# Reordering two products of a seven-product matrix scheme, and one Silu over two PSUM banks in place of two

## The chip, the cores and the metric

The kernel runs on one core of a Trainium2 chip. TensorE (PE) multiplies into PSUM, VectorE (DVE) and ScalarE (ACT) read and write PSUM and SBUF, GpSimd (POOL) works on SBUF alone, and SyncE (SP) issues the DMAs. The engines run side by side. Each takes its own instructions in order, and they wait for each other through semaphores. The metric is the device time of one execution in microseconds (us), as the median of several runs.

## The reference

A bf16 input `x` of 2048 tokens by 512 features is normalised (`xn`). To `x` two things are added: a linear attention over 32 heads of 16 features, and a gated feed-forward block of width 1792. What matters here is the second:

```python
g = silu(xn @ w_gate)
u = xn @ w_up
y = (g * u) @ w_down
```

## The kernel before

The first 512 tokens go through plain matmuls for gate and up (`gu`, line 556). The other 1536 tokens, the part that matters here, go through a scheme with seven products in place of eight (Strassen's, in Winograd's form). The left operand is made of four blocks of the weights (two halves of the contraction of `w_gate` and of `w_up`); the right one is made of four blocks of the input (two halves of the contraction by two halves of 768 tokens). Some products take sums of blocks, made beforehand by DVE (`w_sums`, `x_sum`, line 808).

The loop at line 1132 runs over 14 steps `fc`, each for 128 of the 1792 hidden columns. A step treats the tokens of each block in two halves `q` of `TS` = 384. Each half owns three PSUM banks, `a, b, d = GB[q]`; banks 0 and 1 stay free for other work. A product (`prod`, line 846) is two matmuls of 384 columns into one of these banks. For each half the work is:

- product 1 into `a`; ACT copies `a` to `b` (`seed`, line 856), so that later products add on top of it
- product 5 into `d`; ACT copies `d` to an SBUF tile `p5` (`keep5`, line 861)
- product 2 added into `a`, which then is the gate of the first token block; ACT takes its Silu (`gate(q, 0)`, line 868)
- product 6 added into `b`; DVE writes `b` + `p5` into `d` (`u4`, line 874)
- product 3 added into `d`, the gate of the second block; ACT takes its Silu (`gate(q, 1)`, line 868 too)
- product 7 added into `b`; DVE writes `b` + `p5` to the tile `c22` (`up22`, line 879), and POOL multiplies that with the Silu (`h22`, line 883)
- product 4 added into `b`; DVE multiplies that with the Silu of the first block (`h21`, line 889)

In a step PE takes product 1 of both halves, then 5 of both, then 2, 6, 2, 6 (each half's pair in turn), then 2 fillers (`fill(FA)`), then 3, 7, 3, 7, then 3 fillers (2 in steps 2, 4, 6, 8, 12 and 13; `fill(FB...)`), then 4, 4. A filler is one 512-column matmul of the output of the first 512 tokens (lines 682 and 686).

Each engine's queue is written out in the order of the program text (`K.add`). A helper, `_Program`, finds the waits: an instruction waits for the last writer of all that it reads, and for the last writer and all readers of what it writes. A PSUM bank counts as a whole. So product 2 into `a` waits until `seed` has read `a`, and product 4 into `b` waits until `up22` has read `b`. `seed` of the next step, which writes `b`, waits until `h21` has read it.

After its two Silus of a step ACT has further work before the next step's `seed`: in steps 1 to 9 it scales a slice of `w_gate` or `w_up` (`SC`, line 800), in steps 2 to 7 it also makes a small [128, 1] scalar (`SMALL`, line 780), in steps 10 and 11 it copies part of `w_down` (line 997), and from step 11 it copies pieces of the hidden tile (`hcopy`, line 1055). POOL has, besides `h22`, the products of the attention's division (lines 654, 638), whose results SP turns with DMA transposes.

After step 13 the product with `w_down` uses the same scheme and the same bank triples (`dprod`, line 1083; `attn`, line 1089).

Of the kernel before, what the change touches and what calls it, by code (L numbers as in the profile page):

```python
# [6 lines left out]
ACT = mybir.ActivationFunctionType  # L7
ALU = mybir.AluOpType

P = 128  # L10
# [22 lines left out]
TB = (S - T0) // 2  # L33
TS = TB // 2
# [83 lines left out]
def bass_parallel_sum__linear_attn_block__swiglu_ffn__prompt_kernel(nc, A_x, A_wqkv, A_wo, B_x, B_w_gate, B_w_up, B_w_down, out):  # L118
    xin = A_x[0]
    oview = out[0]  # L120
    K = _Program()
    bf, f32 = dt.bfloat16, dt.float32

    with contextlib.ExitStack() as es:
        E = es.enter_context

        def sb(name, shape, dtype):
            return E(nc.sbuf_tensor(name, shape, dtype))
# [19 lines left out]
        zacc = sb("zacc", [P, 2, D], f32)  # L148
# [35 lines left out]
        sil4 = zacc[:, :, :].rearrange("p a b -> p (a b)").bitcast(bf)[:, 0:4 * TS].rearrange("p (n f) -> p n f", n=4)  # L184
# [12 lines left out]
        c22 = sb("c22", [P, 2, TS], f32)  # L197
# [4 lines left out]
        iw = sb("iw", [P, 2], f32)  # L202
# [8 lines left out]
        sx = sb("sx", [P, 1], f32)  # L211
        iso = sb("iso", [P, 1], f32)
        sm = sb("sm", [P, 1], f32)
        banks = [E(nc.psum_tensor("pb%d" % i, [P, 512], f32)) for i in range(8)]

        def B(i):
            return ("bank", i)
# [48 lines left out]
        for t in range(4, 16):  # L266
# [5 lines left out]
            out=ident[:, :], in_=ident[:, :], compare_op=ALU.not_equal, fill=1.0,  # L272
# [302 lines left out]
        def hj(fc):  # L575
            if fc < 9:
                return hTf[:, fc * HB:(fc + 1) * HB]
            return xnf[:, (fc - 9) * HB:(fc - 8) * HB] if fc < 12 else pqf[:, (fc - 12) * HB:(fc - 11) * HB]

        def hjold(fc):  # L580
            if fc < 9:
                return ph1
            if fc < 12:
                return [("xn", t) for t in range(3 * (fc - 9), 3 * (fc - 8))]
            return [("pq", t) for t in range(3 * (fc - 12), 3 * (fc - 11))]
# [242 lines left out]
                tt("dve", S_[2], A11, A21, ALU.subtract, gk + uk, [("S", n, 2)])  # L828
                tt("dve", S_[3], A12, S_[1], ALU.subtract, gk + [("S", n, 1)], [("S", n, 3)])

        GB = ((2, 3, 4), (5, 6, 7))

        def prod(q, fc, bank, i, start):
            p, o = fc // 2, (fc % 2) * P
            n = p % 2
            cs = slice(fc * P, (fc + 1) * P)
            ts = slice(q * TS, (q + 1) * TS)
            L = {1: wg[:, 0:2, cs], 2: wg[:, 2:4, cs], 4: wu[:, 2:4, cs]}
            lk = {1: ("wgc", fc), 2: ("wgc", fc), 4: ("wuc", fc)}
            for a, b in ((5, 0), (6, 1), (7, 2), (3, 3)):  # L840
                L[a], lk[a] = Sw[:, n, b, :, o:o + P], ("S", n, b)
            R = {1: B11, 2: B21, 3: B22, 4: Tx[3], 5: Tx[0], 6: Tx[1], 7: Tx[2]}
            lo = [("xnT", t) for t in range(4 + 3 * q, 7 + 3 * q)]
            hi = [("xnT", t) for t in range(10 + 3 * q, 13 + 3 * q)]
            rk = {1: lo, 2: lo, 3: hi, 4: [("T", 4)], 5: [("T", 1)], 6: [("T", 2)], 7: [("T", 3)]}
            K.add("pe", [(lambda e, c=c: e.matmul(  # L846
                banks[bank][:, 0:TS], L[i][:, c, :], R[i][:, c, ts], start=(start and c == 0), stop=(c == 1),
                skip_group_check=True)) for c in (0, 1)],
                r=[lk[i]] + rk[i], w=[B(bank)])

        def bk(i):
            return banks[i][:, 0:TS]

        def seed(q, fc):
            a, b, d = GB[q]
            K.add("act", lambda e: e.activation(bk(b), bk(a), ACT.Copy),  # L856
                  r=[B(a)] + ([("sil", 0), ("sil", 1)] if fc == 0 else []), w=[B(b)])

        def keep5(q):
            a, b, d = GB[q]  # L860
            K.add("act", lambda e: e.activation(p5[:, q, :], bk(d), ACT.Copy), r=[B(d)], w=[("p5", q)])

        seen = set()

        def gate(q, i):
            bank = GB[q][0] if i == 0 else GB[q][2]
            n = 2 * q + i
            K.add("act", lambda e: e.activation(sil4[:, n, :], bk(bank), ACT.Silu, scale=iw[:, 0:1]),  # L868
                  r=[B(bank), ("iw",)], w=[("sil4", n), ("zacc", 0), ("zacc", 1)] if n not in seen else [("sil4", n)])
            seen.add(n)  # L870

        def u4(q):
            a, b, d = GB[q]
            K.add("dve", lambda e: e.tensor_tensor(out=bk(d), in0=bk(b), in1=p5[:, q, :], op=ALU.add),  # L874
                  r=[B(b), ("p5", q)], w=[B(d)])

        def up22(q):
            a, b, d = GB[q]
            K.add("dve", lambda e: e.tensor_tensor(out=c22[:, q, :], in0=bk(b), in1=p5[:, q, :], op=ALU.add),  # L879
                  r=[B(b), ("p5", q)], w=[("c22", q)])  # L880

        def h22(q, fc):
            K.add("pool", lambda e: e.tensor_tensor(  # L883
                out=hj(fc)[:, TB + q * TS:TB + (q + 1) * TS], in0=c22[:, q, :], in1=sil4[:, 2 * q + 1, :], op=ALU.mult),
                r=[("c22", q), ("sil4", 2 * q + 1)], w=[("hj", fc, 2 + q)], a=hjold(fc))

        def h21(q, fc):
            b = GB[q][1]
            K.add("dve", lambda e: e.tensor_tensor(
                out=hj(fc)[:, q * TS:(q + 1) * TS], in0=bk(b), in1=sil4[:, 2 * q, :], op=ALU.mult),  # L890
                r=[B(b), ("sil4", 2 * q)], w=[("hj", fc, q)], a=hjold(fc))

        todo = []

# [232 lines left out]
        LATE = {10: [(11, 0)], 11: [(11, 1)]}  # L1127
        SMALL = {i + 2: [fn] for i, fn in enumerate(smalls_d())}
        FA, FB = 2, 3
        DIV = {i: ORDER[i] for i in range(11)}  # L1130
        TURN = {11: (8, 9), 12: (10,)}
        for fc in range(NFC):
            for q in (0, 1):
                prod(q, fc, GB[q][0], 1, True)
                seed(q, fc)
            if fc == 0:
                fill(4)
            for q in (0, 1):
                prod(q, fc, GB[q][2], 5, True)
                keep5(q)  # L1140
            for q in (0, 1):
                prod(q, fc, GB[q][0], 2, False)
                gate(q, 0)
                prod(q, fc, GB[q][1], 6, False)
                u4(q)
            p = fc // 2
            if fc == 0:
                den_sum(DIV[0])
            if fc in DIV:
                den_turn(DIV[fc])  # L1150
            if fc == 1:
                scales_d(1)
            if fc == 12:
                t1_part(0, 1)
                bcopy(22, 1, "pool", [("Tt", 1, 0, 1)])
            if fc == 13:
                t1_part(1, 1)
            fill(FA + (fc == 12))
            for q in (0, 1):
                prod(q, fc, GB[q][2], 3, False)  # L1160
                gate(q, 1)
                prod(q, fc, GB[q][1], 7, False)
                up22(q)
                h22(q, fc)
            fill(FB - (fc in (2, 4, 6, 8, 12)) if fc < 13 else 2)
            if fc == 6:
                oout(1, 1)
            if fc == 0:
                gather_d()
            for q in (0, 1):  # L1170
                prod(q, fc, GB[q][1], 4, False)
                h21(q, fc)
            if p + 1 < NPAIR:
                w_sums(p + 1, fc % 2)
            if fc == 0:
                scale("wu", 2, "pool", [("S", 1, 1)])
            for key, i in SC.get(fc, ()):
                scale(key, i)
            if fc == 0:
                total_d(1)  # L1180
            for fn in SMALL.get(fc, ()):
                fn()
            for n, s_ in LATE.get(fc, ()):
                bcopy(n, s_, "act")
            if fc == 11:
                t1_part(0, 0)
                bcopy(22, 0, "pool", [("Tt", 1, 0, 0)])
            for i in {11: (1,), 12: (0,), 13: (2, 3)}.get(fc, ()):
                hcopy(0, i)
            if fc == 12:  # L1190
                t_sum(2, 0)
                t1_part(1, 0)
                bcopy(21, 0, "pool", [("Tt", 1, 1, 0)])
                bcopy(21, 1, "pool")
            if fc == 13:
                h_sum(0, 0)
                h_sum(0, 1)
                t_sum(2, 1)
            if fc in DIV:
                pq_mul(DIV[fc], [("S", (p + 1) % 2, 1 + 2 * (fc % 2))] if p + 1 < NPAIR else [])  # L1200
                if SLOT[DIV[fc]] < 8:
                    turn(DIV[fc])
                pz_ahead(DIV[fc])
            for i in TURN.get(fc, ()):
                turn(ORDER[i])
            if fc in (9, 10):
                m_scale(fc - 9)
            if fc + 1 in DIV:
                den_sum(DIV[fc + 1])
# [21 lines left out]
        for p in range(NP2 - 1):  # L1231
            a, b, d = GB[p % 2]
# [121 lines left out]
```

## Time and profile before

| | |
|---|---|
| median of 3 runs (lowest, highest) | 200.51 us (200.50, 200.74) |
| the profiled execution, own time | 200.89 us |
| its span, first to last instruction | 199.6 us |
| granted TensorE clock | 1.00 |
| the 14 steps of the loop at line 1132 | 74.88 to 154.16 us |
| in 74.9 to 154.2: PE, DVE, ACT, POOL busy | 78.9, 69.6, 69.2, 57.9 of 79.3 us |

The span is cut into parts by the trace: the attention's projections up to 44.6 us, the plain gate and up products to 74.9 us, the 14 steps to 154.2 us, and the product with `w_down` after that. A busy PE means that some matmul was in flight. Matmuls overlap, so the distance from one matmul's start to the next one's tells more than the busy share. Two matmuls of a product start 0.1625 us apart, each is shown with 0.326 us, so a product takes 0.325 us of PE and its result is there 0.49 us after its start.

### The profile page before, as it was taken

What the parts mean: (1) busy time and instruction counts of PE and PEld (TensorE: products, weight loads), DVE (VectorE), ACT (ScalarE), POOL (GpSimd) and SP (SyncE); (2) the same over time, 40 slices, a digit from 0 to 9 for tenths busy, and PEclk for the clock granted to TensorE, in tenths of its full rate; (3) what the DMA queues carried; (4) which work ended last, traced back from release to release, by engine and by line L of the source; (5) the groups of instructions that cost most, each with busy time, mean ns of one, the idle gap of its engine ahead of it and who ended that gap; (6) DMA issues with size and microseconds to landing.
All of it is one profiled execution on the core that took longest, in us unless ns stands there. A gap on an engine that the chain in (4) does not pass through costs nothing.

```text
span 199.6 us, 3566 instructions
## 1 busy us (share of the span) xinstructions
PE 195.1 (98%) x1193; PEld 114.8 (58%) x1207; DVE 170.5 (85%) x339; ACT 153.6 (77%) x308; POOL 122.3 (61%) x150
## 2 busy tenths in 40 slices
PE   8899999999999999999999999999999999999995
PEld 2344444444544445555555555555555888888884
DVE  2999998894797798988888998887799999998866
ACT  3799887749889988689898988888989968475200
POOL 3687876799995544787677666768877004413220
DMA  6943243289990000011111221000210012132223
GB/s 180 355 122 81 57 87 73 50 282 364 375 295 3 0 3 0 0 28 31 26 26 26 53 56 23 4 0 7 45 34 0 3 39 66 30 79 66 45 69 118
DMA packets 28899, 15.97 MB, mean 80 GB/s; under 512 B 17232, under 2 KB 28880, under 8 KB 28880
## 3 DMA queue, kind: packets, MB, share of 16 engines
q1 hardware_dynamic: 28320, 15.28, 27.3%
q10 hardware_dynamic: 560, 0.46, 0.7%
q8 instruction: 9, 0.15, 0.3%
q14 instruction: 10, 0.08, 0.1%
HBM read 9.70 MB, written 2.10 MB: 59 GB/s over the span
## 4 chain that ended last, share of the span: by engine, by line
PE 94%; DVE 2%; DMA 2%; issue 1%; ACT 0%; POOL 0%; SPq 0%
PE pb L846 32%; PE pb L1083 16%; PE pb L431 13%; PE pb L556 12%; PE pb L480 7%; PE pb L682 6%; PE pb L1089 5%; PE pb L686 2%; DMA x_sb<-in_A_x_dram 2%; PE pb L605 1%; PE pb L674 0%; DVE pq L470 0%; PE pb L398 0%; POOL ef L459 0%; DVE stats L298 0%
## 5 line engine op out<-in xcount | busy, mean ns | idle before, releaser
L654 POOL TENSOR_TENSOR pq<-pq,rden 128x512 bf16<-128x512 bf16 x16 | 16.9, 1056 | 36.7 <-DVE rden L650 23.1
L868 ACT ACTIVATE zacc<-pb,iw 128x384 bf16<-128x384 f32 x56 | 31.3, 590 | 5.9 <-PE pb L846 4.7
L431 PE MATMUL pb<-wqkv,xnT 128*128 128x512 bf16 x110 | 25.1, 379 | 0.2
L846 PE MATMUL pb<-xnT,wg 128*128 128x384 bf16 x112 | 25.1, 326 | 0.0
L638 POOL TENSOR_TENSOR pz<-pq,zbc 128x512 f32<-128x512 bf16 x16 | 18.6, 1164 | 5.3 <-DVE ef L808 3.8
L883 POOL TENSOR_TENSOR hT<-c,zacc 128x384 bf16<-128x384 f32 x18 | 16.1, 915 | 6.0 <-DVE c L879 4.0
L459 POOL TENSOR_SCALAR ef<-ef 128x512 bf16<-128x512 bf16 x25 | 15.5, 620 | 5.8 <-ACT ef L452 5.6
L879 DVE TENSOR_TENSOR c<-pb,p 128x384 f32<-128x384 f32 x28 | 15.5, 555 | 4.1 <-PE pb L846 2.8
L431 PEld LDWEIGHTS pb<-wqkv,xnT 128*128 128x128 bf16 x112 | 10.9, 98 | 13.3 <-DVE pk L470 0.4
L452 ACT ACTIVATE ef<-pb 128x512 bf16<-128x512 f32 x25 | 14.8, 593 | 3.9 <-PE pb L431 3.9
L874 DVE TENSOR_TENSOR pb<-pb,p 128x384 f32<-128x384 f32 x28 | 15.3, 561 | 1.7 <-PE pb L846 0.9
L497 POOL TENSOR_TENSOR zacc<-zacc,pk 128x512 f32<-128x512 f32 x13 | 15.4, 1181 | 1.0
L856 ACT ACTIVATE pb<-pb 128x384 f32<-128x384 f32 x28 | 12.7, 473 | 3.8 <-PE pb L846 2.9
L846 PEld LDWEIGHTS pb<-xnT,wg 128*128 128x128 bf16 x112 | 10.6, 98 | 7.7 <-ACT pb L856 0.8
L556 PE MATMUL pb<-xnT,wg 128*128 128x512 bf16 x56 | 14.7, 379 | 0.0
L556 PE MATMUL pb<-xnT,wu 128*128 128x512 bf16 x53 | 14.3, 379 | 0.1
L846 PE MATMUL pb<-xnT,wqkv 128*128 128x384 bf16 x56 | 13.7, 326 | 0.0
L846 PE MATMUL pb<-GT,wqkv 128*128 128x384 f16 x56 | 13.7, 326 | 0.0
L846 PE MATMUL pb<-wo,wqkv 128*128 128x384 f16 x56 | 13.7, 326 | 0.0
L298 DVE BATCH_NORM_STATS2 stats<-x_sb 128x6 f32<-128x512 bf16 x16 | 10.8, 678 | 3.0 <-DMA x_sb<-in_A_x_dram 3.0
L1089 PE MATMUL pb<-M,pk 128*128 128x256 bf16 x96 | 13.4, 273 | 0.0
L480 PE MATMUL pb<-pk,xn 128*128 128x512 bf16 x55 | 12.5, 379 | 0.1
(210 smaller groups left out, 488.6 us busy)
## 6 DMA issues: line engine op xcount, KB each, us to landing
x_sb<-in_A_x_dram SPq DMA_DIRECT2D x14, 128.0 KB, 4.5
wg<-in_B_w_gate_dram SPq DMA_DIRECT2D x2, 896.0 KB, 8.3
wu<-in_B_w_up_dram SPq DMA_DIRECT2D x2, 896.0 KB, 9.6
wd<-in_B_w_down_dram SPq DMA_DIRECT2D x2, 896.0 KB, 13.7
out_dram<-out_sb SPq DMA_DIRECT2D x24, 64.0 KB, 1.6
wqkv<-in_A_wqkv_dram SPq DMA_DIRECT2D x3, 256.0 KB, 5.0
wqkv<-in_A_wqkv_dram SPq DMA_DIRECT2D x1, 512.0 KB, 9.0
wo<-in_A_wo_dram SPq DMA_DIRECT2D x1, 512.0 KB, 10.0
```

The lines of the kernel that those rows point to most:

```text
L431: K.add("pe", [(lambda e, c=c: e.matmul(banks[b][:, :], src[:, c, t * P:(t + 1) * P], wqkv[:, c, col:col + D], start=(c == 0), stop=(c == ...
L459: K.add("pool", lambda e: e.tensor_scalar(out=buf, in0=buf, scalar1=top, scalar2=0.0, op0=ALU.min, op1=ALU.max), r=[bkey] + tkeys, w=[bkey])
L480: K.add("pe", [(lambda e, c=c: e.matmul(banks[c][:, :], src[:, t, c * P:(c + 1) * P], pk[:, t, :], start=first, stop=last)) for c in range ...
L556: fns.append(lambda e, c=c, b=b, w_=w_: e.matmul(banks[b][:, :], w_[:, c, fc * P:(fc + 1) * P], xnT[:, c, C * 512:(C + 1) * 512], start=(c ...
L638: K.add("pool", lambda e: e.tensor_tensor(out=pzh[i][:, :, 0:DH], in0=heads(pq[:, t, :]), in1=heads(zbc[:, :]), op=ALU.mult), r=[("pq", t) ...
L654: K.add("pool", lambda e: e.tensor_tensor(out=heads(pq[:, t, :]), in0=heads(pq[:, t, :]), in1=rden[:, i, :][:, :, None].broadcast_to([P, N ...
L846: K.add("pe", [(lambda e, c=c: e.matmul(banks[bank][:, 0:TS], L[i][:, c, :], R[i][:, c, ts], start=(start and c == 0), stop=(c == 1), skip ...
L868: K.add("act", lambda e: e.activation(sil4[:, n, :], bk(bank), ACT.Silu, scale=iw[:, 0:1]), r=[B(bank), ("iw",)], w=[("sil4", n), ("zacc", ...
L879: K.add("dve", lambda e: e.tensor_tensor(out=c22[:, q, :], in0=bk(b), in1=p5[:, q, :], op=ALU.add), r=[B(b), ("p5", q)], w=[("c22", q)])
L883: K.add("pool", lambda e: e.tensor_tensor(out=hj(fc)[:, TB + q * TS:TB + (q + 1) * TS], in0=c22[:, q, :], in1=sil4[:, 2 * q + 1, :], op=AL ...
L1083: K.add("pe", [(lambda e, k=k: e.matmul(split(banks[b][:, 0:HD]), L[:, k, :], cut[:, :, k * P:(k + 1) * P], start=(start and k == 0), stop ...
L1089: K.add("pe", [(lambda e, g=g: e.matmul(dk(b), pk[:, SLOT[t], g * P:(g + 1) * P], M[:, g, lo:lo + HD], start=False, stop=(g == NG - 1), sk ...
```

## The change

Three things are done.

The banks are dealt out anew: half 0 has 2, 4, 6 and half 1 has 3, 5, 7, where they had 2, 3, 4 and 5, 6, 7. The eight PSUM tensors of one bank each become one tensor of eight banks, so that an instruction can name two neighbouring ones.

The Silu of the first token block becomes one instruction for both halves (`gate2(0)`), which reads banks 2 and 3 and writes two neighbouring pieces of `sil4`. It stands behind product 2 of half 1. The Silu of the second block stays one for each half (`gate1(q)`). The pieces of `sil4` are numbered anew.

In steps 0 to 11 (`FS = 12`), and in half 1 only (`SWAP = (1,)`), product 7 and `up22` stand ahead of product 3 and its Silu. PE's order there is 3, 7, 7, 3 in place of 3, 7, 3, 7. In steps 12 and 13 it stays.

```diff
-        banks = [E(nc.psum_tensor("pb%d" % i, [P, 512], f32)) for i in range(8)]
+        psum = E(nc.psum_tensor("pb", [P, 8, 512], f32))
+        banks = [psum[:, i, :] for i in range(8)]
...
-        GB = ((2, 3, 4), (5, 6, 7))
+        GB = ((2, 4, 6), (3, 5, 7))
...
+        def gate2(i):
+            lo = GB[0][0] if i == 0 else GB[0][2]
+            K.add("act", lambda e: e.activation(sil4[:, 2 * i:2 * i + 2, :], psum[:, lo:lo + 2, 0:TS], ACT.Silu, scale=iw[:, 0:1]),
+                  r=[B(lo), B(lo + 1), ("iw",)], w=[("sil4", 2 * i), ("sil4", 2 * i + 1)],
+                  a=[("zacc", 0), ("zacc", 1)])
+
+        def gate1(q):
+            d = GB[q][2]
+            K.add("act", lambda e: e.activation(sil4[:, 2 + q, :], bk(d), ACT.Silu, scale=iw[:, 0:1]),
+                  r=[B(d), ("iw",)], w=[("sil4", 2 + q)], a=[("zacc", 0), ("zacc", 1)])
...
+        SWAP = (1,)
+        FS = 12
...
                 prod(q, fc, GB[q][0], 2, False)
-                gate(q, 0)
+                if q:
+                    gate2(0)
                 prod(q, fc, GB[q][1], 6, False)
                 u4(q)
...
-                prod(q, fc, GB[q][2], 3, False)
-                gate(q, 1)
-                prod(q, fc, GB[q][1], 7, False)
-                up22(q)
+                if q in SWAP and fc < FS:
+                    prod(q, fc, GB[q][1], 7, False)
+                    up22(q)
+                    prod(q, fc, GB[q][2], 3, False)
+                    gate1(q)
+                else:
+                    prod(q, fc, GB[q][2], 3, False)
+                    gate1(q)
+                    prod(q, fc, GB[q][1], 7, False)
+                    up22(q)
                 h22(q, fc)
```

More of the change, by code (lines that the diff above doesn't have):

```diff
@@ L861, in keep5 @@
             K.add("act", lambda e: e.activation(p5[:, q, :], bk(d), ACT.Copy), r=[B(d)], w=[("p5", q)])
[L863 to L870, printed above, removed]
+        def gate2(i):
[7 more added lines that the diff above has]
+                  r=[B(d), ("iw",)], w=[("sil4", 2 + q)], a=[("zacc", 0), ("zacc", 1)])
         def u4(q):
@@ L883, in h22 @@
             K.add("pool", lambda e: e.tensor_tensor(
-                out=hj(fc)[:, TB + q * TS:TB + (q + 1) * TS], in0=c22[:, q, :], in1=sil4[:, 2 * q + 1, :], op=ALU.mult),
-                r=[("c22", q), ("sil4", 2 * q + 1)], w=[("hj", fc, 2 + q)], a=hjold(fc))
+                out=hj(fc)[:, TB + q * TS:TB + (q + 1) * TS], in0=c22[:, q, :], in1=sil4[:, 2 + q, :], op=ALU.mult),
+                r=[("c22", q), ("sil4", 2 + q)], w=[("hj", fc, 2 + q)], a=hjold(fc))
         def h21(q, fc):
@@ L889, in h21 @@
             K.add("dve", lambda e: e.tensor_tensor(
-                out=hj(fc)[:, q * TS:(q + 1) * TS], in0=bk(b), in1=sil4[:, 2 * q, :], op=ALU.mult),
-                r=[B(b), ("sil4", 2 * q)], w=[("hj", fc, q)], a=hjold(fc))
+                out=hj(fc)[:, q * TS:(q + 1) * TS], in0=bk(b), in1=sil4[:, q, :], op=ALU.mult),
+                r=[B(b), ("sil4", q)], w=[("hj", fc, q)], a=hjold(fc))
         todo = []
```

## The prediction

> **What bounds the kernel now.** I read the chain that ended last first, then PE's own waits, then the starts of single matmuls and of ACT's instructions around the places that those two views name.
>
> ```profile
> PE 195.1 (98%) x1193; PEld 114.8 (58%) x1207; DVE 170.5 (85%) x339; ACT 153.6 (77%) x308; POOL 122.3 (61%) x150
> ...
> PE 94%; DVE 2%; DMA 2%; issue 1%; ACT 0%; POOL 0%; SPq 0%
> ...
> 97.50 3.25 PE pb L846 x20
> ...
> 102.91 3.32 PE pb L846 x20
> ```
>
> PE carries the chain. Twenty matmuls of the steps take 3.25 us in one place (0.1625 each) and 3.32 in another: the second holds a wait. The 14 steps hold 392 such matmuls (63.70 us) and 69 fillers at 0.216 (14.91), 78.61 together, and they run from 74.88 to 154.16, 79.28 us. So all waits of PE in this stretch are worth 0.67 us, and no change to the order of the steps can give more than that, 0.33% of the time. The pieces "0.05 issue" of the chain are not waits: seven filler matmuls lack a record there (72 of their weight loads are listed in this stretch, and 65 matmuls).
>
> Who makes PE wait, and how ACT stands (the waits in the window 74 to 156 us):
>
> ```profile
> PEld pb L846 <- DVE c L879: 2.1, 8, 0.3
> PEld pb L846 <- DVE pb L874: 1.1, 4, 0.4
> PEld pb L846 <- ACT pb L856: 0.8, 3, 0.3
> ...
> ACT zacc L868 <- PE pb L846: 4.7, 12, 0.6
> ```
>
> These are weight loads that start late, mostly behind matmuls still running, so little of it is lost. By the starts of the matmuls, product 4 of half 1 waits 0.059 us for `up22` (L879) in each of the six steps with two fillers there, 2, 4, 6, 8, 12 and 13. Single waits of 0.03, 0.05 and 0.12 us stand at 110.43, 117.70 and 149.80. ACT is not the bound: it sits idle 4.7 us before Silus until a product is done.
>
> Step 4 on PE, ending with the wait, and that wait itself:
>
> ```profile
> 101.34 0.49 PE L846 MATMUL pb<-wo,wqkv 128*128 128x384 f16 x2
> 101.66 0.49 PE L846 MATMUL pb<-xnT,wqkv 128*128 128x384 bf16 x2
> 101.99 0.49 PE L846 MATMUL pb<-wo,wqkv 128*128 128x384 f16 x2
> 102.31 0.59 PE L682 MATMUL pb<-wd,pk 128*128 128x512 bf16 x2
> 102.75 0.88 PE L846 MATMUL pb<-wqkv,wu 128*128 128x384 f16 x4
> ...
> 103.12 0.11 PEld L846 LDWEIGHTS pb<-wqkv,wu 128*128 128x128 bf16 x2 [0.28 <-DVE c L879]
> ```
>
> From above: product 7 of half 0, product 3 of half 1 (at 101.66), product 7 of half 1 (at 101.99), two fillers, product 4 twice: 0.88 us where other steps show 0.81.
>
> ACT in the same place, and the one place where ACT already holds PE:
>
> ```profile
> 101.54 1.23 ACT L868 ACTIVATE zacc<-pb,iw 128x384 bf16<-128x384 f32 x2 [0.37 <-PE pb L846]
> 102.67 1.14 ACT L800 ACTIVATE wu<-wu,sw 128x1024 bf16<-128x1024 bf16 x1
> 103.71 0.28 ACT L780 ACTIVATE idn<-idn,iw 128x1 f32<-128x1 f32 x1
> 103.99 0.87 ACT L856 ACTIVATE pb<-pb 128x384 f32<-128x384 f32 x2
> ...
> 149.79 0.11 PEld L846 LDWEIGHTS pb<-xnT,wg 128*128 128x128 bf16 x2 [0.34 <-ACT pb L856]
> 149.80 0.50 PE L846 MATMUL pb<-xnT,wg 128*128 128x384 bf16 x2
> ```
>
> The Silu of half 0 starts at 101.54, that of half 1 0.65 later (two products), at 102.19. From there ACT has no gap: scale +0.48, small scalar +1.04, `seed` +0.28, at 103.99. In step 13 ACT's copies made `seed` of half 0 start at 149.265 and end at 149.744; product 2, which overwrites the bank that this seed reads, started at 149.80 where 149.68 was its turn. So the rule for what follows, from that row: product 2 starts at its turn or 0.055 after the seed's end, and a seed lasts 0.475.
>
> **The change, part by part.**
>
> *Banks and the single tensor.* A product, copy or add takes the same number of columns in another bank. At the start of step 0 the banks now used first were freed earlier (the last readers of banks 5 and 7, L593, end at 74.3 and 75.8; new use of 7 is product 5, after four fillers, at 76.7). In the `w_down` part the triples are renamed throughout. Cost zero; the reused banks give no bound but a few hundredths either way.
>
> *The wide Silu.* It removes 14 instructions of 0.590 and makes 14 longer. Its duration is in no row. Ends: 0.59 (as one of today's) and 1.18 (as two). I take 0.92: 0.590 plus 384 elements at 0.84 ns (L800 with 1024 elements took 1.138 and L997 with 896 took 1.031), nearest to both rows. It must wait for product 2 of half 1 (in step 4: started 99.93, done 100.42), where today the first of the two need not. Queued behind it are the Silus of the second block; the first of these waits for its product until 101.54 anyway. The room from 100.46 is 1.08 us, so 0.92 fits; 1.18 overruns by 0.1, and is caught up, since the last Silu's data come 0.98 after (below). Its readers, `h21`, run at 103.27 and later; its banks are written again at the next step. So at either end it costs and gains nothing on the path: what it saves on ACT, 14 x (0.464 - 0.32) = 2.0 us at the spacing of two Silus today, becomes idle time ahead of L868.
>
> *The swap, gain.* `up22` of half 1 (second of "x2" in L879's rows) starts 0.65 after that of half 0, at 102.51 in step 4, and ends at 103.07. With its product one place earlier it has its data at 102.15 and follows `up22` of half 0 at DVE's spacing of 0.46, from 102.33 to 102.88. Product 4's turn is 103.07, so the wait goes, with 0.011 of a slowed first matmul after it: 0.07 us in each of steps 2, 4, 6 and 8, 0.28 in all. Steps 12 and 13 keep theirs. `u4` of half 1 is waited for by whichever product comes third, at the same time as today. DVE's order is unchanged, POOL's `h22` of half 1 is queued behind that of half 0 (0.87 apart) and starts no later. No DMA moves, and SP and POOL are passed by nothing.
>
> *The swap, loss.* Product 3 of half 1 comes one product later, so its Silu starts 0.98 after half 0's instead of 0.65: 0.325 later, in every step up to 11. Behind it on ACT stand scale, small scalar or copies, and then the seed that product 2 of the next step waits for. With S the start of a step, product 2 has its turn at S + 1.30, so the seed may start up to S + 0.77; today it starts at S + 0.53 where ACT is free. Step by step, with the present starts and +0.325:
>
> Step 4 to 5: seed at 104.315 (103.99 + 0.325), ends 104.79, product 2 at 104.845. Its turn is 104.77 today and 104.695 with the wait of step 4 gone: 0.15 lost, with the slowed matmul 0.16. Step 6 to 7: ACT free at 115.142 today, 115.467 then; product 2 at 115.997 against a turn of 115.848: 0.16. Step 2 to 3, with a small scalar of 0.19 only: seed at 93.11, product 2 at 93.64 against 93.58: 0.07. Step 11 to 12, two copies and no gap (141.262, 141.74, 142.67, 143.285): seed at 143.61, product 2 at 144.143 against 143.984: 0.17. Elsewhere the seed still fits, with 0.10 (1 to 2), 0.15 (3 to 4), 0.09 (5 to 6), 0.07 (7 to 8) and 0.13 us (8 to 9) to spare; steps 0, 9 and 10 have more. Losses: 0.56 us. As PE is late in step 7, the wait for `u4` at 117.70 (0.06 with its slowed matmul) falls away.
>
> Sum: -0.28 - 0.06 + 0.56 = +0.22 us. Against the profiled execution's own 200.89 us (1.3 of it outside the span) that is 201.11; that execution stands 0.38 above the median of the runs, so the median goes from 200.51 to 200.73.
>
> What a waiting weight load costs enters every wait here. The row at 149.80 has its matmul start 0.005 us behind the load's start. The Trainium skill (TensorE: Matmul & The Clock Gate, LDWEIGHTS) gives a load 128 / 1.2 = 107 ns, which would stand in the open if a matmul had to follow its load's end: five waits removed and four added would each weigh 0.1 more, and the sum, an estimate, would be +0.12. The same page (Architectural detail) lets a matmul begin before its weights are all in, and the trace agrees with its 0.005.
>
> **The rivals.**
>
> *The seed comes later still (slower).* The place is ACT between the last Silu and the seed of steps 1 to 9. In step 2 the second seed began at 88.14, 0.37 after the last work it waits for (`h21`, ended 87.77), which I can't explain; lateness of that kind on the first seed decides from 0.07 us on, the smallest spare. At 0.1 more in each step, four waits grow by 0.1 and the steps with 0.07 and 0.09 to spare add 0.03 and 0.01: +0.44, 201.17 us. For it: ACT has no gap there. Against it: the spacings are the same in all steps to 0.01.
>
> *ACT's lateness is harmless.* If product 2 didn't wait for the seed as at 149.80, only the gains stay: -0.28, 200.23 us, with 117.70 -0.06, 200.17. Against it: 110.43 shows the same wait (seed ended 110.370, matmul 0.055 later).
>
> *ACT is the bound.* Then its 2.0 us come off: 198.5 us. Against it: 4.7 us idle ahead of L868, and the bound of 0.67 us on all of PE's waits. By the Trainium skill (ScalarE: Activation LUTs, What ACT_TABLE_LOAD costs) an activation with one pointer operand has about 0.28 us fixed, of which some 0.09 overlap with the next; by that, an estimate, 14 x 0.19 = 2.6 us would come off. No trace row here separates the fixed part.
>
> **How the numbers follow.** The forecast has 0.46 (200.6 to 200.9), the later seed 0.37 (200.9 to 201.6; every one of my spares is small, and errors on ACT add up in one direction), the harmless seed 0.12 (200.1 to 200.6), the bound on ACT 0.05. A measurement of this kernel tells about 0.2% (0.4 us) from no change. Forecast and harmless seed lie within that: 0.58. Slower 0.37, faster 0.05. The range reaches from the harmless seed, 200.2, to the later seed with 0.12 us in place of 0.1 (4 x 0.12, and 0.05 and 0.03 in the two steps with the least to spare: +0.56), 201.3; beyond it lie about 0.07 below and 0.1 above.
>
> **What would show it.** In the changed trace: Silus of 128x768 at 0.92 us, with idle time ahead of the next Silu; PE's waits for L879's line down from eight to about four; `up22` pairs 1.02 long instead of 1.21; PE's waits for `seed` up from three, near the starts of steps 3, 5, 7 and 12, 0.07 to 0.17 each; the 14 steps 79.5 us long instead of 79.28. I am wrong if the last Silu of a step does not start 0.98 after the one ahead of it, if those four waits are missing, or if the stretch before 74.9 or after 154.2 changes its length.

## The result and the profile after

| | before | changed |
|---|---|---|
| median of 14 runs | 200.62 us | 200.99 us |
| lowest, highest | 200.41, 201.18 | 200.89, 201.76 |
| profiled execution, span | 199.65 us | 199.74 us |
| the 14 steps in that trace | 79.11 us | 79.52 us |
| from the last step's end to the last instruction | 45.82 us | 45.87 us |

The ratio is 1.0023, with a 95% interval of 1.0014 to 1.0031: slower, by about 0.4 us. The two spans differ by less, since the first step began at 74.72 us in one profile and at 74.35 in the other, all of it ahead of anything that the change touches. Over the profiles shown below this start lies anywhere from 74.31 to 74.84 whatever the kernel. So from here on the 14 steps are compared, from the start of the first matmul of step 0 to the start of the last of step 13. (The 79.28 us of the table ahead is the same stretch before the change, counted there from the second matmul's start to the last one's end.) There the change costs +0.407 us, and the stretch behind them adds 0.05.

The page of the changed kernel: PE's share is as before, ACT has 14 instructions less, and the wide Silu lasts 0.900 us.

```profile
PE 195.0 (98%) x1193; PEld 114.7 (57%) x1207; DVE 170.0 (85%) x339; ACT 152.0 (76%) x294; POOL 121.9 (61%) x150
...
PE 94%; DVE 2%; DMA 1%; issue 1%; ACT 0%; POOL 0%; SPq 0%
...
L866 ACT ACTIVATE zacc<-pb,iw 128x768 bf16<-128x768 f32 x14 | 12.6, 900 | 2.4 <-PE pb L847 2.0
```

The waits of the changed kernel, 74 to 156 us. Its lines stand a little lower in the file: L857 is `seed`, L872 the Silu of 384, L877 `u4`, L882 `up22`.

```profile
ACT zacc L872 <- PE pb L847: 7.5, 26, 0.4
...
PEld pb L847 <- ACT pb L857: 1.7, 6, 0.4
PEld pb L847 <- DVE c L882: 1.7, 5, 0.7
PEld pb L847 <- DVE pb L877: 1.1, 4, 0.4
```

The waits for `seed` (L857) went from 3 to 6. Those for `up22` (L882) went from 8 to 5, but one of the five is 0.7 us long, where the longest was 0.3. ACT's waits ahead of Silus went from 4.7 us to 7.5, and 2.0 more ahead of the wide ones. Most of that comes from the swap: in the run below with the swap alone they are 8.7 us, in the one with the wide Silu alone 5.8. By the pages ACT is busy 1.6 us less (153.6 and 152.0), and none of it reaches the time.

Step 4 on PE and on ACT in the changed kernel, for comparison with the same step before:

```profile
100.90 0.81 PE L847 MATMUL pb<-wo,wqkv 128*128 128x384 f16 x4
101.55 0.49 PE L847 MATMUL pb<-xnT,wqkv 128*128 128x384 bf16 x2
101.88 0.59 PE L683 MATMUL pb<-wd,pk 128*128 128x512 bf16 x2
102.31 0.81 PE L847 MATMUL pb<-wqkv,wu 128*128 128x384 f16 x4
102.96 0.81 PE L847 MATMUL pb<-xnT,wg 128*128 128x384 bf16 x4
103.61 0.81 PE L847 MATMUL pb<-ef,wqkv 128*128 128x384 f16 x4
104.31 0.50 PE L847 MATMUL pb<-xnT,wg 128*128 128x384 bf16 x2
```

```profile
101.10 0.58 ACT L872 ACTIVATE zacc<-pb,iw 128x384 bf16<-128x384 f32 x1 [0.18 <-PE pb L847]
102.08 0.58 ACT L872 ACTIVATE zacc<-pb,iw 128x384 bf16<-128x384 f32 x1 [0.39 <-PE pb L847]
102.56 1.14 ACT L801 ACTIVATE wu<-wu,sw 128x1024 bf16<-128x1024 bf16 x1
103.60 0.28 ACT L781 ACTIVATE idn<-idn,iw 128x1 f32<-128x1 f32 x1
103.78 0.85 ACT L857 ACTIVATE pb<-pb 128x384 f32<-128x384 f32 x2
```

Both products 7 now stand together (0.81, four matmuls), product 3 of half 1 follows at 101.55, and product 4 takes 0.81 where it took 0.88: the wait for `up22` is gone. The Silus are 0.98 apart (101.10, 102.08) where they were 0.65. Behind the second, scale, small scalar and seed follow without a gap, and in step 5 product 2 stands at 104.31 where its turn was 104.26: a wait for the seed has come.

That much was foreseen. What was not lies in step 13, where the order of products is the old one. PE of the changed kernel, and then DVE and POOL of the changed kernel:

```profile
152.47 0.59 PE L683 MATMUL pb<-wd,pk 128*128 128x512 bf16 x2
153.23 0.96 PE L847 MATMUL pb<-wqkv,wu 128*128 128x384 f16 x4 [0.17 <-DVE c L882]
```

```profile
151.41 1.29 DVE L1013 SCALAR_TENSOR_TENSOR mixb<-wd,sd,wg 128x384 f16<-128x384 bf16 x1
152.63 1.01 DVE L882 TENSOR_TENSOR c<-pb,p 128x384 f32<-128x384 f32 x2
```

```profile
150.31 2.00 POOL L1001 TENSOR_SCALAR wu<-wd,sd 128x896 bf16<-128x896 bf16 x2 [1.25 <-DVE mixb L1013]
```

The same two engines before the change:

```profile
151.79 0.62 DVE L1010 SCALAR_TENSOR_TENSOR mixb<-wd,sd,wg 128x384 f16<-128x384 bf16 x1
152.39 1.21 DVE L879 TENSOR_TENSOR c<-pb,p 128x384 f32<-128x384 f32 x2
```

```profile
150.83 2.37 POOL L998 TENSOR_SCALAR wu<-wd,sd 128x896 bf16<-128x896 bf16 x2 [1.24 <-DVE mixb L1010]
```

DVE's `t1_part(1, 1)` (L1010, now L1013) makes a piece of a sum of `w_down` blocks, and POOL's second `bcopy(21, ...)` (L998, now L1001) copies another block of `w_down`. They run at the same time and need nothing from each other, yet one of them is always stretched. Before, DVE started at 151.787 and POOL's second copy at 151.821, 0.034 later: DVE's piece lasted 0.62 us and POOL's copy 1.38 in place of 1.01. After, POOL started at 151.291 and DVE at 151.413, 0.122 later: POOL's copy lasted 1.01 and DVE's piece 1.29 in place of 0.62. So the one that starts second pays, though not for the whole overlap: POOL lost 0.37 us where the two had overlapped for 0.59, DVE lost 0.67 where they had overlapped for 0.89. DVE's loss pushes both `up22`, and product 4 waits for them: 0.334 us ahead of half 0 and 0.128 ahead of half 1, where only 0.059 stood before.

The order tipped because of step 12. PE waited 0.161 us there for the late seed. DVE's `t1_part(1, 1)` is queued behind `u4` and so behind PE, and it took on that delay. POOL's two copies follow DVE's earlier `t1_part(1, 0)`, which did not. So DVE came 0.16 later against POOL: -0.034 became +0.122. Why `t1_part(1, 0)` kept its place shows best in the run below with the swap in step 11 alone, where nothing was gained ahead of step 12. DVE before the change, and then DVE of that run:

```profile
149.13 0.94 DVE L1019 TENSOR_TENSOR wg<-wu,mixb 128x896 f16<-128x896 bf16 x1
150.00 0.74 DVE L1010 SCALAR_TENSOR_TENSOR mixb<-wd,sd,wg 128x512 f16<-128x512 bf16 x1
```

```profile
149.04 0.80 DVE L1022 TENSOR_TENSOR wg<-wu,mixb 128x896 f16<-128x896 bf16 x1
149.76 0.74 DVE L1013 SCALAR_TENSOR_TENSOR mixb<-wd,sd,wg 128x512 f16<-128x512 bf16 x1
```

Counted from the first matmul of step 0, the sum ahead of `t1_part(1, 0)` (`t_sum(2, 0)`, first line of each) starts 0.169 us later in that run, with PE, but ends only 0.024 later, since it lasts 0.80 in place of 0.94. It overlaps POOL's second `h22` of step 12, which is queued behind other work on POOL and ends only 0.025 later. In all ten profiles the sum ends 0.48 us after that `h22` does, whether it started early or late. So, by these rows, POOL held DVE up there already, and the late start was absorbed.

Summed up over the steps, by the starts of the matmuls (waits of PE in us):

| where | before | changed |
|---|---|---|
| product 4, half 1, in steps 2, 4, 6, 8 (for `up22`) | 4 x 0.06 | 0 |
| step 7, product 3 (for `u4`) | 0.051 | 0.029 |
| steps 5, 7, 12, product 2 (for `seed`) | 0 | 0.055, 0.054, 0.161 |
| step 12, product 4 (for `up22`) | 0.061 | 0.061 |
| step 13, product 2 (for `seed`) | 0.118 | 0.118 |
| step 13, product 4 (for `up22`) | 0.059 | 0.334 and 0.128 |
| step 6, product 2 (for `seed`) | 0.031 | 0.031 |
| ahead of step 1, a matmul of one column (L767, now L768), no wait | 0.026 | 0.026 |

The columns add up to 0.585 and 0.997 us: +0.41, which is the whole of the 0.407.

### The profile page after: what moved, and what is told of

Its sections match the earlier page's. It is cut to its first block, busy times and chain, and to the rows that moved or that the text cites. A ratio compares the mean times of both kernels' runs of the same rounds, so it can differ in the third digit from the quotient of the medians.

```text
span 199.7 us, 3540 instructions
## 1 busy us (share of the span) xinstructions
PE 195.0 (98%) x1193; PEld 114.7 (57%) x1207; DVE 170.0 (85%) x339; ACT 152.0 (76%) x294; POOL 121.9 (61%) x150
## 4 chain that ended last, share of the span: by engine, by line
PE 94%; DVE 2%; DMA 1%; issue 1%; ACT 0%; POOL 0%; SPq 0%
PE pb L847 32%; PE pb L1086 16%; PE pb L432 13%; PE pb L557 12%; PE pb L481 7%; PE pb L683 6%; PE pb L1092 5%; PE pb L687 2%; DMA x_sb<-in_A_x_dram 1%; PE pb L606 1%; PE pb L675 0%; DVE pq L471 0%; POOL ef L460 0%; DVE stats L299 0%; ACT ef L453 0%
## 5 line engine op out<-in xcount | busy, mean ns | idle before, releaser
L872 ACT ACTIVATE zacc<-pb,iw 128x384 bf16<-128x384 f32 x28 | 16.3, 581 | 7.7 <-PE pb L847 7.5
L882 DVE TENSOR_TENSOR c<-pb,p 128x384 f32<-128x384 f32 x28 | 14.3, 550 | 3.1 <-PE pb L847 3.0
L877 DVE TENSOR_TENSOR pb<-pb,p 128x384 f32<-128x384 f32 x28 | 15.4, 562 | 1.6 <-PE pb L847 0.9
L866 ACT ACTIVATE zacc<-pb,iw 128x768 bf16<-128x768 f32 x14 | 12.6, 900 | 2.4 <-PE pb L847 2.0
L857 ACT ACTIVATE pb<-pb 128x384 f32<-128x384 f32 x28 | 12.5, 470 | 1.1 <-PE pb L847 0.9
```

The source lines that it names most:

```text
L872: K.add("act", lambda e: e.activation(sil4[:, 2 + q, :], bk(d), ACT.Silu, scale=iw[:, 0:1]), r=[B(d), ("iw",)], w=[("sil4", 2 + q)], a=[(" ...
```

## The experiments

The theory: the time comes from the later last Silu alone, through the seeds of steps 5, 7 and 12, and through step 12's wait that lets POOL ahead of DVE in step 13. The main rival: the wide Silu, the new banks or the single tensor cost it.

**The wide Silu and the banks without the swap.**

```diff
-        FS = 12
+        FS = 0
```

> The changed kernel without the swap: new banks, one PSUM tensor and the wide Silu stay. Theory 1 (the time comes from the last Silu's lateness, and from POOL's copy overtaking DVE's in step 13): as before, 200.6 us, ratio 0.9995 to 1.0005; PE's six waits of 0.06 for up22 are back, the wait of 0.33 ahead of product 4 in step 13 is gone. Rival (the wide Silu or the banks cost it): 200.8 to 201.0, with the wait in step 13 still there.

Measured: 200.61 us against 200.66 before, ratio 0.9999 (0.9989 to 1.0009). The steps take 79.101 us against 79.114, with the six waits for `up22` back and each other wait within 0.003 us of before. The wide Silu and the banks cost and bring nothing. The rival falls.

**The swap without the wide Silu and the banks.** The kernel before, with the `if q == 1 and fc < 12` branch and the old `gate`.

> The kernel before with the swap of steps 0 to 11 alone: old banks, two Silus of 384. Theory 1: as the changed kernel, +0.37 us (200.9 to 201.1), with seed waits of about 0.05, 0.05 and 0.16 at steps 5, 7 and 12 and a long wait in step 13. Rival: about -0.2 us, since only the four removed waits are left.

Measured: 201.01 us, ratio 1.0021 (1.0012 to 1.0030). The steps take 79.521 us, the same as in the whole change to 0.001, with waits of 0.058, 0.057 and 0.159 at steps 5, 7 and 12 and 0.340 and 0.130 in step 13. The swap is the whole of it.

**The swap in steps 0 to 10.**

```diff
-        FS = 12
+        FS = 11
```

> The changed kernel with the swap in steps 0 to 10 only. Theory 1: step 12 starts without its wait of 0.16, so DVE's part in step 13 starts ahead of POOL's copy again (by 0.03 us before the change, so this could tip either way): 0.57 us less than the changed kernel, 200.4 us; if it tips, 200.8. Rival (step 13's wait has nothing to do with step 12's): 200.8 us with the wait of 0.33 still there.

Measured: 200.46 us, ratio 0.9995 (0.9986 to 1.0005). The steps take 78.934 us, 0.587 less than in the changed kernel and 0.18 less than before. With step 11 left as it was, product 2 of step 12 has no wait and DVE is ahead again in step 13. DVE's rows and then POOL's of this run:

```profile
151.63 0.65 DVE L1013 SCALAR_TENSOR_TENSOR mixb<-wd,sd,wg 128x384 f16<-128x384 bf16 x1
152.23 1.21 DVE L882 TENSOR_TENSOR c<-pb,p 128x384 f32<-128x384 f32 x2
```

```profile
150.70 2.38 POOL L1001 TENSOR_SCALAR wu<-wd,sd 128x896 bf16<-128x896 bf16 x2 [1.24 <-DVE mixb L1013]
```

**The swap in step 11 alone.**

```diff
-                if q in SWAP and fc < FS:
+                if q in SWAP and fc == 11:
```

> The changed kernel with the swap in step 11 alone. Theory 1: the wait of 0.16 at step 12 and the long one in step 13 (0.33 + 0.13) come from this one swap, with nothing gained against them: the 14 steps take 79.11 + 0.17 + 0.40 = 79.68 us, and the time is 201.2 us, more than that of the whole change. Rival (all twelve swaps add to it, or chance): 200.7 us.

Measured: 201.25 us, ratio 1.0026 (1.0012 to 1.0041), the steps 79.712 us (79.68 expected). Waits of 0.160 at step 12, and 0.347 and 0.129 in step 13. One swapped pair out of twelve costs 0.60 us, more than the whole change, which had its gains against it. DVE, POOL and PE of this run (POOL's second copy starts at 151.592, DVE's piece at 151.701):

```profile
151.70 1.31 DVE L1013 SCALAR_TENSOR_TENSOR mixb<-wd,sd,wg 128x384 f16<-128x384 bf16 x1
```

```profile
150.60 2.01 POOL L1001 TENSOR_SCALAR wu<-wd,sd 128x896 bf16<-128x896 bf16 x2 [1.24 <-DVE mixb L1013]
```

```profile
153.53 0.96 PE L847 MATMUL pb<-wqkv,wu 128*128 128x384 f16 x4 [0.18 <-DVE c L882]
```

**POOL's copy put behind DVE's piece**, in the changed kernel. This takes the overlap away and leaves all else.

```diff
             if fc == 13:
                 t1_part(1, 1)
+                bcopy(21, 1, "pool", [("Tt", 1, 1, 1)])
...
                 bcopy(21, 0, "pool", [("Tt", 1, 1, 0)])
-                bcopy(21, 1, "pool")
```

> The changed kernel, with POOL's last copy of w_down made to wait for DVE's last t1_part. Theory 1: t1_part's second piece of step 13 lasts 0.62 us in place of 1.29, the waits ahead of product 4 in step 13 shrink from 0.33 and 0.13 to 0 and 0.06, and the time falls by 0.4 us to 200.6; the waits at steps 5, 7 and 12 stay. Rival (step 13 waits for something else): 1.29 us stays or the time stays at 201.0.

Measured: 200.84 us, ratio 1.0008 (0.9999 to 1.0017). DVE, and then POOL:

```profile
151.44 0.61 DVE L1013 SCALAR_TENSOR_TENSOR mixb<-wd,sd,wg 128x384 f16<-128x384 bf16 x1
```

```profile
152.14 1.01 POOL L1001 TENSOR_SCALAR wu<-wd,sd 128x896 bf16<-128x896 bf16 x1 [0.79 <-DVE mixb L1013]
153.12 0.91 POOL L886 TENSOR_TENSOR pq<-c,zacc 128x384 bf16<-128x384 f32 x1
```

In the steps it went as expected: the piece lasts 0.61 us, the long waits are gone, and the steps take 79.105 us, 0.416 less. So the overlap with POOL's copy is what stretched DVE's piece. But the time is 200.84 us and not the 200.6 expected: in the trace only 0.19 us of the 0.42 is left at the end. The stretch behind the steps grew by 0.23, to 46.09 us, with two new waits of PE, 0.06 at 155.12 and 0.18 at 159.24. The rows of that stretch that lead there:

```profile
PEld pb L1092 <- ACT pb L1098: 0.4, 1, 0.4
DVE xn L1070 <- ACT xn L1058: 0.3, 1, 0.3
ACT xn L1058 <- POOL pq L886: 0.3, 1, 0.3
PEld pb L1086 <- DVE pb L1112: 0.3, 1, 0.3
```

The later copy leaves POOL's `h22` of step 13 at 153.12, where in the changed kernel it stood at 153.26. Counted from the first matmul of the steps, PE had won 0.42 there, POOL only 0.17. An ACT copy of the hidden tile (L1058) and DVE's sums behind it (L1070) wait for that `h22`; they too are 0.17 earlier, and PE meets them in the first products with `w_down`. The gain was met by the next wait in the row.

**The small scalars moved into ACT's idle time**, with the swap in steps 0 to 10.

```diff
+            for fn in SMALL.get(fc, ()):
+                fn()
             p = fc // 2
...
-            for fn in SMALL.get(fc, ()):
-                fn()
```

> The swap in steps 0 to 10, and ACT's small scalar of steps 2 to 7 moved from behind the last Silu to ahead of the first Silu of the second block, where ACT sits idle. Theory 1 (the seed is late because the last Silu is 0.325 us later and scale and small scalar stand behind it): PE's waits for the seed at steps 5 and 7 (0.055 each) vanish, the stretch of the 14 steps shortens from 78.93 to 78.80 us, time 200.35 us. Rival (product 2 waits there for something else): the 0.055 stay, 200.46 us.

Measured: 200.39 us against 200.73 before, ratio 0.9984 (0.9974 to 0.9994); the steps take 78.875 us (78.80 expected). ACT and PE of this run at the same place as above:

```profile
100.78 0.28 ACT L781 ACTIVATE idn<-idn,iw 128x1 f32<-128x1 f32 x1
101.06 0.58 ACT L872 ACTIVATE zacc<-pb,iw 128x384 bf16<-128x384 f32 x1
102.04 0.58 ACT L872 ACTIVATE zacc<-pb,iw 128x384 bf16<-128x384 f32 x1 [0.39 <-PE pb L847]
102.52 1.14 ACT L801 ACTIVATE wu<-wu,sw 128x1024 bf16<-128x1024 bf16 x1
103.56 0.85 ACT L857 ACTIVATE pb<-pb 128x384 f32<-128x384 f32 x2
```

```profile
103.57 0.81 PE L847 MATMUL pb<-ef,wqkv 128*128 128x384 f16 x4
104.22 0.49 PE L847 MATMUL pb<-xnT,wg 128*128 128x384 bf16 x2
```

The seed follows the scale at once, and step 5 has no wait: product 2 at 104.22 stands in its turn. At step 7 the wait shrank from 0.054 to 0.031 only, and the wait of product 3 there is back at 0.05, where the changed kernel had 0.029. What is left ahead of product 2 is a seed held by DVE: step 6 has an output add ahead of `h21`. Step 5 has one too, and the wait of 0.03 at step 6 stays in every run. So the queue behind the last Silu is what made the seeds late, and this version is the one that beats both kernels: the swap pays 0.06 us in each of four steps once next to nothing hangs on the late Silu (0.24 us less than before the change).

**The same 0.06 us won without the swap.** The kernel before, with a filler moved from ahead of products 3 and 7 to behind them in the six steps that wait.

```diff
-            fill(FA + (fc == 12))
+            fill(FA + (fc == 12) - (fc in (2, 4, 6, 8, 12, 13)))
...
-            fill(FB - (fc in (2, 4, 6, 8, 12)) if fc < 13 else 2)
+            fill(FB)
```

> The kernel before, products in their old order: in steps 2, 4, 6, 8, 12 and 13 one filler matmul goes from ahead of the products 3 and 7 to behind them, which gives up22 the 0.216 us that it lacks, and makes both last Silus 0.216 earlier. Theory 1 (PE's six waits for up22 are all there is to win, and a late last Silu is what the swap pays with): six times 0.07 less, 200.2 us, steps 78.7 us, no new wait for u4 (about 0.05 to spare) or for the seed. Rival (products 3 now wait for u4): 200.6 us, waits of 0.05 or more ahead of product 3.

Measured: 200.62 us, ratio 0.9995 (0.9972 to 1.0017), the steps 79.094 us. The rival was right. Waits for `up22` fell from eight to two, waits for `u4` rose from four to ten:

```profile
PEld pb L846 <- DVE pb L874: 3.0, 10, 0.4
PEld pb L846 <- ACT pb L856: 0.7, 3, 0.2
PEld pb L846 <- DVE c L879: 0.4, 2, 0.2
```

In steps 4 and 8 nothing took the place of the wait removed. In steps 2, 6, 12 and 13 product 3 stood 0.167, 0.141, 0.048 and 0.097 us late, since DVE came to `u4` late there. The 0.05 us to spare held in steps 4 and 8 and in none of those four. The waits for the seed changed too: the wait of 0.118 at product 2 of step 13 is gone, since the seed there begins 0.075 earlier (counted from the first matmul) and PE comes later, and a wait of 0.03 came at step 7. All that was won was lost again but for 0.02 us.

**That with the wide Silu and the banks** (`FS = 0` and the fillers moved).

> As the run before, with the new banks and the wide Silu, and no swap. Theory 1 (the wide Silu's saving ends as ACT's idle time): the same as without it, 200.2 us. Rival (the wide Silu pays once PE waits for nothing else): 0.1 us or more less than without it.

Measured: 200.83 us, ratio 1.0014 (0.9991 to 1.0036), the steps 79.105 us against 79.094. The time is inconclusive with that interval. By the trace the wide Silu again changes nothing: the waits are those of the run before, to 0.01.

## Why the prediction was right in kind and where it was not

The ratio of 1.0023 lies in the stated range and on the side of the sum, but just over the bound of 0.2%: the likeliest case said +0.22 us, measured were about +0.4. The time lies among those given to the rival of a later seed (200.9 to 201.6) and not in the forecast's own range (200.6 to 200.9). Step by step:

- *Banks and the single tensor, zero*: right, shown by the run without the swap.
- *The wide Silu, 0.92 us and no effect*: right. It lasts 0.900, and the steps with it alone take 0.013 us less than without.
- *The swap's gain, 0.07 us in each of four steps*: right, all four waits are gone. They are worth 0.06 each, so 0.24 in place of 0.28.
- *Step 11 to 12, 0.17 us*: right, 0.161 and the slowed matmul.
- *Steps 4 to 5 and 6 to 7, 0.16 each*: the mechanism was right and the size was off, 0.055 and 0.054. The step that failed is "small scalar +1.04, `seed` +0.28". The seed began 0.28 after the small scalar before the change, but it was waiting for its product, which came at just that moment. With the product long done the seed begins 0.186 after it (103.596 to 103.782), while the scalar's row still runs. So ACT was 0.10 us less late than put.
- *Step 2 to 3, 0.07*: for the same reason no wait at all (the seed begins 0.093 after the start of a small scalar of 0.192). Of the four waits for `seed` whose absence was to show an error, this one is missing.
- *Step 7, 0.06 gained*: about a third of that, as PE was 0.1 us less late there.
- *Elsewhere the seed still fits*: right, at 1 to 2, 3 to 4, 5 to 6, 7 to 8 and 8 to 9.
- *Steps 12 and 13 "keep theirs"*: wrong for step 13, and the largest single term, +0.40 us. The working treated a wait of PE in one step as a shift of all that follows. POOL's copies did not shift with PE, and a pair of instructions 0.034 us apart changed places. The sum had no term for two engines that slow each other without waiting for each other.

Two misses partly cancelled: 0.28 us too much at steps 3, 5 and 7, and 0.40 too little in step 13. That the sum came as near as it did is luck in that respect. The rival of a later seed has the measured time in its range with the wrong cause: the seeds came earlier than put, not later. That ACT's lateness is harmless, and that ACT is the bound, are both refuted by the runs with the swap alone and without it.

## What to carry to other kernels

Where an engine stands at 98%, list its waits by the starts of its instructions and sum them; no more than that can come of a reordering there, and each move must be followed to what is queued behind the instruction that comes later. Don't take a delay as a shift of everything: look for pairs of instructions on two engines that run at the same time and whose starts are close, since a delay on one side can change their order. An interval between two rows is a price only if the second was ready earlier; where it was waiting for data, the engine's own spacing can be shorter (here 0.186 us in place of 0.28).

## What the runs showed of the hardware

A DVE instruction with two SBUF inputs and a POOL copy slow each other, and the later one pays. In the nine profiles in which the two overlap in step 13, the one that started first ran in its own time (0.62 to 0.65 us for DVE's piece, 1.01 to 1.02 for POOL's copy), and the other, started 0.03 to 0.20 us later, took longer: DVE 1.29 to 1.31, POOL 1.31 to 1.39. The Trainium skill (SBUF — State Buffer, Who interferes with whom) says that a DVE instruction with two SBUF inputs contends with a POOL instruction that reads SBUF, and that the order of issue decides which of them is held up. The trace agrees. The prediction had not looked for it, since neither instruction was part of the change.

An activation behind another one begins before the first one's row ends: 0.186 us behind a [128, 1] activation of 0.281, so an overlap of 0.095. The Trainium skill (ScalarE: Activation LUTs, What ACT_TABLE_LOAD costs) gives about 93 ns, and the trace agrees.
